# TensorE order within a slot: the output product between gate and value, and unit outputs behind the multiplication

## Chip, cores and metric

The kernel runs on one core of a Trainium2 chip. The metric is the time of one execution on the device in microseconds (us). Where two kernels are compared, the ratio is the mean time of one kernel's fast runs over that of the other's of the same rounds, so it is not quite the ratio of the medians quoted beside it.

## The reference

An attention block with 32 learned queries is followed by a gated feed-forward block; the second one takes nearly all of the time.

```python
h = mab(I, x)                    # 32 inducing rows attend to 12416 rows, 4 batches
x = mab(x, h)                    # every row attends to the 32 rows of h
rms = sqrt(mean(x * x, -1) + 1e-6); xn = x / rms * rms_g
g = xn @ w_gate                  # 128 -> 1536
silu = g / (1 + exp(-g))
val = xn @ w_val                 # 128 -> 1536
out = (silu * val) @ w_out       # 1536 -> 128, 49664 rows
```

## The kernel before

The rows are cut into 100 units of at most 512 columns, and each unit into 12 slots (`j`), one for each 128 of the 1536 channels. A slot makes a gate and a value product on TensorE (single-pass `float32r`), a silu on ScalarE, a multiplication `u` on VectorE, and one output product of some earlier slot. An output product is either plain (`float32`, which TensorE runs as two passes: 1598 matmul records for 799 products) or split into three single passes, for which ScalarE and GpSimd make `hi`, `lo` and `d`. Attention work of the next batch is spread over the slots as planned steps.

```python
ps_gv = pool("ps_gv", 4, space=PSUM)      # gate and value products share four banks
...
def project(lhsT, rhs):
    nc.tensor.matmul(acc[:, 0:T], lhsT, rhs, start=..., stop=...)
    st["left"] -= 1
    if not st["left"]:                     # last output product of the unit
        o = ...
        nc.vector.tensor_tensor(out=o, in0=acc, in1=o, op=ALU.add)      # shortened
        nc.vector.transpose(out=o[:, 0:T], in_=...)
        soon(2, lambda: store(o))
...
for j in range(NJ):
    g = ps_gv.tile(...); nc.tensor.matmul(g, sg[:, ts(j, P)], a)        # L597
    v = ps_gv.tile(...); nc.tensor.matmul(v, sv[:, ts(j, P)], a)        # L599
    sl = silp.tile(...); nc.scalar.activation(sl, g, AF.Silu)           # L601
    t = up.tile(...);    nc.vector.tensor_tensor(out=t, in0=sl, in1=v)  # L603
    slot(j)            # steps that are due, planned steps, then one or two output products
```

A planned step splits the rows of a stack into two halves, all on VectorE:

```python
nc.vector.transpose(out=aT[rows, 0:w], in_=sc[b][rows, cols2[s]])       # L500
nc.vector.tensor_copy(out=hi[rows, 0:w], in_=aT[rows, 0:w])             # L502
nc.vector.tensor_tensor(out=lo, in0=aT, in1=hi, op=ALU.subtract)        # L503
```

## Time and profile before

| | before |
|---|---|
| time, median of 3 runs | 1718.8 us (1718.05 to 1718.83) |
| TensorE busy | 1680.2 us, 98% of the span |
| VectorE, ScalarE, GpSimd busy | 70%, 70%, 69% |
| quiet slot with a plain output product | 1.327 us |
| quiet slot with a split output product | 1.16 us |

The first row is what is measured without a profile; the rest is from one profiled execution. TensorE's busy share alone does not prove that it is the bound, since a busy matmul row can hold queueing.

### The profile page before, as it was taken

Reading aid. Unit: us, or ns where it says so; the run is one execution under the profiler, and the core shown is the slowest. Engines: PE = TensorE matmul, PEld = TensorE weight load, DVE = VectorE, ACT = ScalarE, POOL = GpSimd, SP = SyncE. Lnnn points to the kernel's source line nnn. Section 1 sums busy time; section 2 is a strip of 40 time slices with the busy share of each in tenths; the row PEclk is TensorE's granted clock in tenths of the full one; section 3 lists DMA queues with packets and bytes.
Section 4 is the critical chain, followed back from the end, with each engine's and each line's share of the span. In section 5 each row is a group of like instructions: output and inputs, shape, how many; then the busy total and the mean of one; then the engine's idle time right before and its main releaser. Section 6 shows DMA issues by size and latency. Waiting matters only on the chain.

```text
span 1716.6 us, 23555 instructions
## 1 busy us (share of the span) xinstructions
PE 1680.2 (98%) x6855; PEld 1045.7 (61%) x6855; DVE 1201.7 (70%) x1982; ACT 1207.7 (70%) x2180; POOL 1179.0 (69%) x936
## 2 busy tenths in 40 slices
PE   9899999999999999999999999999999999999998
PEld 7545565655566656665656656565556666666666
DVE  4867876777578776667667877667757666766665
ACT  4347777676677777766777777767677777787776
POOL 0317775777487776676657877577647888888875
PEclk9999999999999999999999999999999999999999
DMA  6344433434343232434434324153211121121121
GB/s 248 86 68 74 72 78 71 110 77 70 55 80 62 50 67 47 105 76 90 68 58 83 55 37 84 41 121 79 51 30 34 33 37 31 33 36 36 32 36 24
DMA packets 389360, 112.66 MB, mean 66 GB/s; under 512 B 365136, under 2 KB 369776, under 8 KB 386672
## 3 DMA queue, kind: packets, MB, share of 16 engines
q1 hardware_dynamic: 388944, 111.02, 32.3%
q8 instruction: 54, 0.88, 0.2%
q14 instruction: 74, 0.61, 0.1%
q10 hardware_dynamic: 288, 0.15, 0.0%
HBM read 53.95 MB, written 27.00 MB: 47 GB/s over the span
## 4 chain that ended last, share of the span: by engine, by line
PE 91%; ACT 3%; DVE 2%; issue 2%; DMA 1%; POOL 1%; ACTq 0%; DVEq 0%; POOLq 0%
PE acc L550 42%; PE gv L599 16%; PE gv L597 16%; PE u L563 5%; PE u L565 5%; PE mm L301 3%; ACT silu L601 1%; PE mm L478 1%; DVE u L603 1%; PE mm L358 1%; DMA xn<-in_x_dram 1%; PE acc L178 1%; ACT L601 1%; PE gv L358 0%; PE mm L430 0%
## 5 line engine op out<-in xcount | busy, mean ns | idle before, releaser
L603 DVE TENSOR_TENSOR u<-silu,gv 128x512 f32<-128x512 f32 (+2 forms) x1200 | 785.7, 665 | 444.6 <-ACT silu L601 378.3
L601 ACT ACTIVATE silu<-gv 128x512 f32<-128x512 f32 (+2 forms) x1200 | 699.5, 585 | 414.7 <-PE gv L597 357.9
L550 PE MATMUL acc<-u,wo 128*128 128x512 f32 (+2 forms) x1598 | 797.3, 583 | 0.1
L597 PE MATMUL gv<-a,sg 128*128 128x512 f32 (+2 forms) x1200 | 768.3, 640 | 14.6 <-ACT silu L601 6.6
L585 POOL TENSOR_TENSOR xn<-u,xn 128x512 fp32r<-128x512 f32 (+2 forms) x401 | 505.9, 1262 | 309.7 <-ACT xn L584 250.0
L590 POOL TENSOR_TENSOR xn<-hs,xn 128x512 fp32r<-128x512 f32 (+2 forms) x401 | 507.8, 1266 | 74.0 <-POOL xn L585 25.6
L599 PE MATMUL gv<-a,sv 128*128 128x512 f32 (+2 forms) x1200 | 475.7, 396 | 5.2 <-DVE u L603 3.3
L597 PEld LDWEIGHTS gv<-a,sg 128*128 128x128 f32 x1200 | 227.6, 190 | 223.4 <-issue 140.5
L599 PEld LDWEIGHTS gv<-a,sv 128*128 128x128 f32 x1200 | 228.1, 190 | 214.5 <-issue 125.7
L550 PEld LDWEIGHTS acc<-u,wo 128*128 128x128 f32 x1598 | 295.4, 189 | 93.5 <-issue 33.8
L584 ACT ACTIVATE xn<-u 128x512 fp32r<-128x512 f32 (+2 forms) x401 | 245.7, 613 | 17.6 <-DVE u L603 16.0
L589 ACT ACTIVATE hs<-xn 128x512 f32<-128x512 f32 (+2 forms) x401 | 246.3, 614 | 7.1 <-POOL xn L590 6.9
L563 PE MATMUL u<-xn,xn 128*128 128x512 f32 (+2 forms) x401 | 167.9, 419 | 0.0
L550 PE MATMUL acc<-xn,xn 128*128 128x512 f32 (+2 forms) x401 | 156.1, 389 | 2.4 <-POOL xn L590 2.4
L565 PE MATMUL u<-xn,xn 128*128 128x512 f32 (+2 forms) x401 | 155.4, 387 | 0.0
L563 PEld LDWEIGHTS u<-xn,xn 128*128 128x128 f32 x401 | 75.2, 188 | 43.2 <-issue 26.3
L492 POOL TENSOR_TENSOR rs<-ms,mhalf 128x16 f32<-128x16 f32 (+2 forms) x28 | 75.5, 2698 | 36.2 <-DVE ms L490 35.7
L565 PEld LDWEIGHTS u<-xn,xn 128*128 128x128 f32 x401 | 75.4, 188 | 19.1 <-issue 5.2
L550 PEld LDWEIGHTS acc<-xn,xn 128*128 128x128 f32 x401 | 75.3, 188 | 18.8 <-POOL xn L590 2.9
L555 DVE TENSOR_TENSOR o<-acc,o 128x512 f32<-128x512 f32 (+2 forms) x97 | 65.1, 671 | 21.7 <-ACT o L568 18.9
L556 DVE STREAM_TRANSPOSE o<-o 128x512 f32<-128x512 f32 (+2 forms) x97 | 67.7, 698 | 3.3
L568 ACT ACTIVATE o<-u 128x512 f32<-128x512 f32 (+2 forms) x97 | 56.4, 582 | 19.0 <-PE u L565 16.7
(155 smaller groups left out, 758.0 us busy)
## 6 DMA issues: line engine op xcount, KB each, us to landing
out_dram<-o SPq DMA_DIRECT2D x320, 64.0 KB, 2.0
xT<-in_x_dram SPq DMA_DIRECT2D x60, 256.0 KB, 4.5
xn<-in_x_dram SPq DMA_DIRECT2D x60, 256.0 KB, 4.7
a<-hi SPq DMA_DIRECT2D x160, 64.0 KB, 2.0
a<-lo SPq DMA_DIRECT2D x158, 64.0 KB, 2.0
w<-w SPq DMA_DIRECT2D x22, 256.0 KB, 3.3
xn<-in_x_dram SPq DMA_DIRECT2D x5, 1024.0 KB, 11.2
out_dram<-o SPq DMA_DIRECT2D x64, 60.0 KB, 2.0
```

Of the source, the lines that this page charges most:

```text
L492: nc.gpsimd.tensor_tensor(out=rs, in0=ms, in1=mhalf[rows, 0:n], op=ALU.pow)
L550: nc.tensor.matmul(acc[:, 0:T], lhsT, rhs, start=st["left"] == NJ, stop=st["left"] == 1)
L563: nc.tensor.matmul(ups[:, 0:T], w[:, i, :], hi, start=st["k"] == nk, stop=False)
L565: nc.tensor.matmul(ups[:, 0:T], w[:, NK + i, :], lo, start=False, stop=not st["k"])
L584: nc.scalar.activation(hi, v, AF.Copy, scale=1.0 - 2.0 ** -13)
L585: nc.gpsimd.tensor_tensor(out=lo, in0=v, in1=hi.bitcast(F32), op=ALU.subtract)
L589: nc.scalar.activation(hs[:, 0:T], hi.bitcast(F32), AF.Copy, scale=2.0 ** -12)
L590: nc.gpsimd.tensor_tensor(out=d, in0=hs[:, 0:T], in1=lo.bitcast(F32), op=ALU.subtract)
L597: nc.tensor.matmul(g[:, 0:T], sg[:, ts(j, P)], a[:, 0:T], start=True, stop=True)
L599: nc.tensor.matmul(v[:, 0:T], sv[:, ts(j, P)], a[:, 0:T], start=True, stop=True)
L601: nc.scalar.activation(sl[:, 0:T], g[:, 0:T], AF.Silu)
L603: nc.vector.tensor_tensor(out=t[:, 0:T], in0=sl[:, 0:T], in1=v[:, 0:T], op=ALU.mult)
```

## The change

The intent is to start the value product as late as its multiplication can use it: the silu takes about 0.6 us, and meanwhile the output product runs, so the value product sits in its PSUM bank for a shorter time. For this `slot` is parted in two: `products` (the output products) comes between gate and value, `steps` (all else) after the multiplication. The addition and transpose that end a unit would then stand on VectorE ahead of the slot's own multiplication, so they are put off to the `steps` that follow.

```diff
-                o = st["o"] if nk else outp.tile([P, 512], F32, name="o")
-                if nk:
-                    nc.vector.tensor_tensor(...)
-                nc.vector.transpose(...)
-                soon(2, lambda: store(o))
+                soon(1, finish)
+
+        def finish():
+            ... # the same lines
@@
             nc.tensor.matmul(g[:, 0:T], sg[:, ts(j, P)], a[:, 0:T], start=True, stop=True)
+            sl = silp.tile([P, 512], F32, name="silu")
+            nc.scalar.activation(sl[:, 0:T], g[:, 0:T], AF.Silu)
+            products(j)
             v = ps_gv.tile([P, 512], F32, name="gv", tag="gv")
             nc.tensor.matmul(v[:, 0:T], sv[:, ts(j, P)], a[:, 0:T], start=True, stop=True)
-            sl = silp.tile([P, 512], F32, name="silu")
-            nc.scalar.activation(sl[:, 0:T], g[:, 0:T], AF.Silu)
             t = up.tile([P, 512], F32, name="u")
             nc.vector.tensor_tensor(out=t[:, 0:T], in0=sl[:, 0:T], in1=v[:, 0:T], op=ALU.mult)
-            slot(j)
+            steps(j)
```

(`slot` becomes `steps`, which runs what is due and what is planned, and `products`, whose counting is unchanged.) `soon(1, ...)` reads as "a slot later", which is misleading here: `finish` is registered by `products(j)` and runs in `steps(j)` of the same slot, with the steps that are due and so ahead of those that are planned.

More of the change, by code (lines that the diff above doesn't have):

```diff
@@ L535, in split_wo, with ffn @@
             kws[name] = xnp.tile([P, 4, 512], F32R, name=f"xn{full - 4 + k}")
-    def ffn(b, u, slot):
+    def ffn(b, u, products, steps):
         s, q = units[u]
@@ L552, in project @@
             if not st["left"]:
-                o = st["o"] if nk else outp.tile([P, 512], F32, name="o")
-                if nk:
-                    nc.vector.tensor_tensor(out=o[:, 0:T], in0=acc[:, 0:T], in1=o[:, 0:T], op=ALU.add)
-                nc.vector.transpose(out=o[:, 0:T], in_=(o if nk else acc)[:, 0:T])
-                soon(2, lambda: store(o))
+                soon(1, finish)
+        def finish():
+            o = st["o"] if nk else outp.tile([P, 512], F32, name="o")
+            if nk:
+                nc.vector.tensor_tensor(out=o[:, 0:T], in0=acc[:, 0:T], in1=o[:, 0:T], op=ALU.add)
+            nc.vector.transpose(out=o[:, 0:T], in_=(o if nk else acc)[:, 0:T])
+            soon(2, lambda: store(o))
         def project3(j, hi, lo, d):
@@ L795, with steps @@
         for u in range(NU):
-            def slot(j):
+            def steps(j):
                 k = u * NJ + j
-                now = b * NU * NJ + k
                 for one in waiting:
                     one[0] -= 1
-                for one in [one for one in waiting if not one[0]]:
+                while any(not one[0] for one in waiting):
+                    one = next(one for one in waiting if not one[0])
                     waiting.remove(one)
@@ L812, in slot, with products @@
                     gather(*after[b, u])
+            def products(j):
+                k = u * NJ + j
+                now = b * NU * NJ + k
                 count = max(len(plain) - 1, 0) + sum(at <= now for at, _ in kara)
@@ L823, in slot @@
                         plain.pop(0)()
-            ffn(b, u, slot)
+            ffn(b, u, products, steps)
     while kara or plain:
         (plain.pop(0) if plain else kara.pop(0)[1])()
-    for _, step in waiting:
-        step()
+    while waiting:
+        waiting.pop(0)[1]()
 _INS = ['x', 'inducing', 'moe_w_gate', 'moe_w_val', 'moe_w_out', 'moe_rms_g']
```

## The prediction

> **What bounds the kernel now.** I read the page first: busy shares, then the chain that ended last, then the costliest groups.
>
> ```profile
> PE 1680.2 (98%) x6855; PEld 1045.7 (61%) x6855; DVE 1201.7 (70%) x1982; ACT 1207.7 (70%) x2180; POOL 1179.0 (69%) x936
> ...
> PE 91%; ACT 3%; DVE 2%; issue 2%; DMA 1%; POOL 1%; ACTq 0%; DVEq 0%; POOLq 0%
> ...
> L603 DVE TENSOR_TENSOR u<-silu,gv 128x512 f32<-128x512 f32 (+2 forms) x1200 | 785.7, 665 | 444.6 <-ACT silu L601 378.3
> ...
> L597 PE MATMUL gv<-a,sg 128*128 128x512 f32 (+2 forms) x1200 | 768.3, 640 | 14.6 <-ACT silu L601 6.6
> ...
> L599 PE MATMUL gv<-a,sv 128*128 128x512 f32 (+2 forms) x1200 | 475.7, 396 | 5.2 <-DVE u L603 3.3
> ```
>
> TensorE is busy for 98% of the span and carries 91% of the last chain; no other engine is over 70%. VectorE's 378.3 us of waiting for the silu lies on an engine that is not the bound. A busy matmul row can still hide waits, so I looked at a quiet stretch of the timeline.
>
> ```profile
> 805.36 1.02 PE L550 MATMUL acc<-u,wo 128*128 128x512 f32 x2
> ...
> 805.82 0.80 PE L597 MATMUL gv<-a,sg 128*128 128x512 f32 x1
> ...
> 806.46 0.40 PE L599 MATMUL gv<-a,sv 128*128 128x512 f32 x1
> ...
> 806.69 1.02 PE L550 MATMUL acc<-u,wo 128*128 128x512 f32 x2
> ...
> 807.15 0.80 PE L597 MATMUL gv<-a,sg 128*128 128x512 f32 x1
> ```
>
> From gate to gate a slot takes 807.15 - 805.82 = 1.33 us. The value product starts 0.23 us before the output product, which has two passes. By unrounded starts each pass lasts 0.429 and gate and value 0.235 each: 2 x 0.429 + 2 x 0.235 = 1.328. The sum fills the slot, so TensorE streams without a hole. (The gate's row starts early and reads 0.80 because it is queued behind the second output pass.) With a split output product (L563, L565, L550, three single passes) five single passes take 1.16 us.
>
> How much of the run is not like this? I took all value-product starts from the trace and grouped the slots by what TensorE runs in them. The 530 plain slots of width 512 last 707.7 us in all and are together 4.9 us longer than if each had the group's 10th percentile; the 264 split ones last 318.5 us, excess 12.3. Over all slots, real waiting comes to about 57 us: 18 before 142 us (the weights are being prepared), about 21 around the two long exponentials of each of three batches, 6 in the four narrow units (256 columns), 8.5 in ten stalls of 0.6 to 0.9 us, and the rest in slots without an output product. Of the ten stalls this is one:
>
> ```profile
> 1374.21 1.66 DVE L503 TENSOR_TENSOR lo<-aT,hi 128x512 fp32r<-128x512 f32 x1
> ...
> 1375.79 2.58 DVE L603 TENSOR_TENSOR u<-silu,gv 128x512 f32<-128x512 f32 x4
> ...
> 1376.52 0.50 PE L597 MATMUL gv<-a,sg 128*128 128x512 f32 x1 [0.65 <-DVE u L603]
> ```
>
> VectorE was held by a slow split (1.66 us), the multiplications queued behind it, and TensorE found no free bank. Such stalls are what the change can shorten.
>
> **What the Trainium skill says.** "TensorE: Matmul & The Clock Gate", section Step-by-step, says that matmuls stay in program order while weight loads are pulled ahead of running matmuls. The trace agrees: weight loads of 0.19 us lie beside the stream (PEld 61% busy). So an order of products costs nothing by itself if the same kinds of pass follow one another. Its section Back-to-back issue gap gives about 216 ns for 512 columns; this trace has 235 for a single pass and 429 for each fp32 pass, and I use these. "PSUM — Partial Sum Buffer", Specifications, has 8 banks per partition; the kernel takes all (4 gate and value, 2 accumulators, 1 + 1), so the change has only the order in which to relieve a bank. "GPSIMD Engine Reference", Specifications, says that its SBUF interfaces are shared with VectorE when VectorE has two SBUF inputs; the 1.66 us split, which takes 0.69 elsewhere in this trace (at 265.41), fits.
>
> **The change part by part.** It adds and removes no arithmetic instruction.
>
> 1. *TensorE order.* Before: gate, value, two output passes. After: gate, two output passes, value. In steady state both are the same cycle: two single passes, then two fp32 passes; only the names of the single ones change places. I expect 1.33 and 1.16 us a slot again. Change: 0.
>
> 2. *The value bank is held shorter.* In the trace the silu starts 0.43 us after its gate, where the gate was not queued, and takes 0.60: it ends 1.03 us after the gate starts. The multiplication starts 0.83 us (median) after the value product does (0.43 would do if the silu were there). Before: value at 0.235, multiplication 1.07 to 1.75, so the bank is held 1.5 us. After: value at 0.235 + 0.86 = 1.09, multiplication 1.52 to 2.2, bank held 1.1 us. The next use of a bank, two slots on, is at 2 x 1.33 + 0.235 = 2.9 before and 3.75 after: slack goes from 1.1 to 1.5 us. Of ten stalls totalling 8.5 us I take off about 0.4 us each, with some gone: about -5 us. After an exponential the first value product no longer stands behind the multiplication (about 0.25 us, six times): -1 us.
>
> 3. *Less slack from a multiplication to its output product.* The product is issued 0.235 us earlier relative to its gate and the multiplication ends 0.4 to 0.45 us later: 0.65 us less, and up to 1.2 us less where attention products are in the slot, as those now come after the output product. I followed the kernel's own queue: plain products run 2 slots behind 41 times, 3 slots 485 times, 4 or more 271 times; split ones 5 or 6 behind. In the trace the slack from multiplication to product has a median of 2.8 us, 5th percentile 0.94, 1st 0.39. Shifting each by these amounts makes 26 plain products late by 7 us together; most follow an exponential, when the queue is drained. The split products' GpSimd result has slack 0.67 at the 5th percentile; shifting makes three newly late by 0.5 us each. Around 130 to 137 us TensorE already waits for GpSimd, and the value product now stands behind that wait: +0.5. Together about +6 us, of which a part replaces a wait that is there anyway: +4.
>
> 4. *Unit outputs.* 97 units have an addition (671 ns) and a transpose (698 ns). They go ahead of the planned steps rather than after them, and behind the last value product's multiplication. The 1.4 us on VectorE stay; they delay the next multiplication by about 0.7 us instead of 0.55, within the new slack. Change: 0.
>
> Sum: 0 - 6 + 4 + 0 = -2 us; from 1718.8 that is about 1717.
>
> **The rivals.**
>
> *A real gain.* If the shorter hold also dissolved the stalls of the exponentials and the narrow units, 8.5 + 6 + half of 21 could go: 25 us, 1694 us (1.5%). For it: many weight loads wait for silu or multiplication. Against it: most of these waits are 0.24 us long, under a running fp32 pass, and behind an exponential TensorE waits for ScalarE, which stays blocked as long, with the same number of banks ahead of it. Over 2% is 34 us; that needs more waits than I can find.
>
> *A new wait.* Gate and value banks come from one pool of four, and 201 of the 1200 gate weight loads wait for VectorE (value banks), not for ScalarE. For these the multiplication now ends at 2.2 us and the gate is due at 2.65, in split slots at 2.32; the load must be clear 0.2 us before. If more gates drew such banks, each could lose 0.1 to 0.2 us: 200 of them 20 to 40 us, 1740 to 1755 us. Against it: banks are handed out as they come free, and the silu's comes first.
>
> *VectorE becomes the bound.* It has 70% now and gets no new work, but the multiplication is no longer ready until the slot's end. If transposes wait behind it, attention steps slip. With 30% idle and planned steps several slots apart I give it 5 us at most.
>
> **Range and chances.** The terms are -6 and +4, each uncertain by about its own size, and the engines' contention shifts by a few us whenever order changes. Repeated times lie within 0.8 us, so noise adds nothing. I take 1716, slightly under the start, and 1704 to 1729 for 8 in 10. Outside the 2% band: 0.04 faster, 0.03 slower.
>
> **What would show it.** In quiet stretches the slot should stay at 1.33 and 1.16 us; another figure makes step 1 wrong. The value row should read about 0.80 us in the mean rather than 0.40, and the gate row 0.40: queueing only. VectorE's wait before the multiplication should be laid to the value product (PE) instead of the silu. Ten stalls near 199, 614, 1027 and 1375 to 1685 us should shrink to 0.5 or vanish (step 2). Output products should show short waits for VectorE after the exponentials near 277, 452, 691 and 866 us (step 3). The prediction fails if the quiet slot changes, or if gate weight loads wait for VectorE's multiplication far more than the 22.3 us that the view of waits has now.

## The result, and the profile after

The changed kernel takes 1717.7 us (median of 4 runs, 1717.4 to 1718.2), the kernel before 1718.4 in its runs up to then (4, 1715.7 to 1718.8). The ratio is 1.000 with a 95% interval of 0.998 to 1.002: the same time.

Two rows of the page before are needed for comparison, those of the output products (plain, then the last product of a split one):

```profile
L550 PE MATMUL acc<-u,wo 128*128 128x512 f32 (+2 forms) x1598 | 797.3, 583 | 0.1
...
L550 PE MATMUL acc<-xn,xn 128*128 128x512 f32 (+2 forms) x401 | 156.1, 389 | 2.4 <-POOL xn L590 2.4
```

The page of the changed kernel, busy shares and costliest groups (the columns are busy us and mean ns, then the idle time of the engine before them and what ended most of it):

```profile
PE 1675.3 (98%) x6855; PEld 1046.2 (61%) x6855; DVE 1189.4 (69%) x1982; ACT 1222.4 (71%) x2180; POOL 1181.4 (69%) x936
...
L607 DVE TENSOR_TENSOR u<-silu,gv 128x512 f32<-128x512 f32 (+2 forms) x1200 | 788.2, 665 | 471.9 <-PE gv L605 276.6
...
L550 PE MATMUL acc<-u,wo 128*128 128x512 f32 (+2 forms) x1598 | 793.9, 581 | 7.0 <-DVE u L607 5.8
L605 PE MATMUL gv<-a,sv 128*128 128x512 f32 (+2 forms) x1200 | 768.1, 640 | 1.3 <-ACT silu L602 0.7
...
L600 PE MATMUL gv<-a,sg 128*128 128x512 f32 (+2 forms) x1200 | 492.5, 410 | 14.3 <-ACT silu L602 6.5
...
L550 PE MATMUL acc<-xn,xn 128*128 128x512 f32 (+2 forms) x401 | 159.0, 396 | 6.2 <-POOL xn L593 5.9
```

Gate and value have changed rows: the value's row now reads 640 ns, the gate's 410. That is queueing behind the second output pass, not work. VectorE's longest wait is laid to the value product instead of the silu. TensorE's idle time before gate and value is 15.6 us (19.8 before), but output products, which hardly waited before (0.1 and 2.4 us), now wait 7.0 and 6.2 us. By these rows idle time rose from 22.3 to 28.8 us, while TensorE's busy time fell by 4.9 us; as busy rows hold queueing, the page alone doesn't say what was won or lost.

A quiet stretch of the changed kernel's timeline (start and duration in us, then engine and line):

```profile
804.84 0.40 PE L600 MATMUL gv<-a,sg 128*128 128x512 f32 x1
...
805.07 1.02 PE L550 MATMUL acc<-u,wo 128*128 128x512 f32 x2
...
805.11 0.69 DVE L607 TENSOR_TENSOR u<-silu,gv 128x512 f32<-128x512 f32 x1 [0.84 <-PE gv L605]
...
805.53 0.80 PE L605 MATMUL gv<-a,sv 128*128 128x512 f32 x1
...
806.17 0.40 PE L600 MATMUL gv<-a,sg 128*128 128x512 f32 x1
```

From gate to gate it is 806.17 - 804.84 = 1.33 us, as before. The order is another, the stream is as full.

To see where the few us went I took the end of every slot's gate product in both traces and watched the difference (changed less before) grow along the slots. The numbers are in us; a minus is a gain.

| slots of a batch | where | batches 0, 1, 2 |
|---|---|---|
| 0 to 48 of the first batch | weights are being prepared | -0.86 |
| 132 to 144 | first long exponential | -0.25, -0.26, -0.23 |
| 192 to 204 | planned products | -0.45, -0.46, -0.46 |
| 204 to 216 | a split product waits for GpSimd | +0.74, +0.74, +0.74 |
| 228 to 240 | a split product waits for GpSimd | +0.90, +0.89, +0.90 |
| 252 to 264 | second long exponential | -1.80, -0.55, -1.59 |
| 0 to 12 of the next batch | | -0.35, -0.39, -0.31 |

These sum to -3.1 us, losses of 4.9 included. The other stretches add 1.2 up to slot 1188, in steps of under 0.3, and the end of the program 0.9. The spans differ by 1.0 (1716.65 and 1715.69).

### The profile page after: what moved, and what is told of

Same layout as the page of the kernel before. It is cut to its first block, busy times and chain, and to the rows that moved or that the text cites. A ratio compares the mean times of both kernels' runs of the same rounds, so it can differ in the third digit from the quotient of the medians.

```text
span 1715.7 us, 23430 instructions
## 1 busy us (share of the span) xinstructions
PE 1675.3 (98%) x6855; PEld 1046.2 (61%) x6855; DVE 1189.4 (69%) x1982; ACT 1222.4 (71%) x2180; POOL 1181.4 (69%) x936
## 5 line engine op out<-in xcount | busy, mean ns | idle before, releaser
L605 PE MATMUL gv<-a,sv 128*128 128x512 f32 (+2 forms) x1200 | 768.1, 640 | 1.3 <-ACT silu L602 0.7
L593 POOL TENSOR_TENSOR xn<-hs,xn 128x512 fp32r<-128x512 f32 (+2 forms) x401 | 507.0, 1264 | 53.4 <-POOL xn L588 16.7
L600 PE MATMUL gv<-a,sg 128*128 128x512 f32 (+2 forms) x1200 | 492.5, 410 | 14.3 <-ACT silu L602 6.5
L550 PEld LDWEIGHTS acc<-u,wo 128*128 128x128 f32 x1598 | 299.1, 189 | 87.5 <-issue 17.9
L568 PE MATMUL u<-xn,xn 128*128 128x512 f32 (+2 forms) x401 | 155.8, 388 | 0.0
L566 PE MATMUL u<-xn,xn 128*128 128x512 f32 (+2 forms) x401 | 155.4, 388 | 0.0
L566 PEld LDWEIGHTS u<-xn,xn 128*128 128x128 f32 x401 | 75.3, 188 | 15.6
```

The source lines that it names most:

```text
L550: nc.tensor.matmul(acc[:, 0:T], lhsT, rhs, start=st["left"] == NJ, stop=st["left"] == 1)
L566: nc.tensor.matmul(ups[:, 0:T], w[:, i, :], hi, start=st["k"] == nk, stop=False)
L568: nc.tensor.matmul(ups[:, 0:T], w[:, NK + i, :], lo, start=False, stop=not st["k"])
L593: nc.gpsimd.tensor_tensor(out=d, in0=hs[:, 0:T], in1=lo.bitcast(F32), op=ALU.subtract)
L600: nc.tensor.matmul(g[:, 0:T], sg[:, ts(j, P)], a[:, 0:T], start=True, stop=True)
L605: nc.tensor.matmul(v[:, 0:T], sv[:, ts(j, P)], a[:, 0:T], start=True, stop=True)
```

## The experiments

Each kernel ran five rounds (the two with three banks ran three) beside the kernel before, which had a median of 1718.07, 1717.91 and 1717.96 us in the three calls. By the verdicts' mark of 2% every run with four banks is "the same" as the kernel before; the smaller differences below rest on the intervals in brackets. A comparison with the changed kernel itself (1717.7) is one across calls.

### The order alone

```diff
-                soon(1, finish)
+                finish()
```
(in the changed kernel)

> The new TensorE order alone; the unit's addition and transpose stay right behind the last output product, so on VectorE they now come before that slot's multiplication. Theory (TensorE is a full stream, the order is worth nothing, and a multiplication has slack): 97 multiplications end about 0.5 us later than in the changed kernel, 2.7 + 0.7 = 3.4 us after their gate against a bank need at 3.75 (3.2 in split slots), so 0 to 10 us longer than the changed kernel, 1717 to 1728. Rival (moving the unit outputs gave back what the order cost, so the order alone is clearly slower): over 1735.

It took 1722.6 us (1721.7 to 1722.8), ratio to the kernel before 1.0025 (1.0012 to 1.0037). The estimate holds: 4.9 us over the changed kernel. By the difference of gate ends to the changed kernel the losses come late in each of three batches: 1.06 us in slots 236 to 248, 0.4 around and behind the second exponential (up to slot 272), 0.7 in the last units (up to 296). Earlier in each batch some is won back (0.5 at slots 132 to 144, 0.3 at 228 to 240). In the page output products wait for the multiplication 8.9 us instead of 5.8. So the putting-off of unit outputs is a necessary part of the change.

### The unit outputs alone

```diff
-                o = ...   # addition, transpose and store of the unit, at once
+                soon(1, finish)
```
(in the kernel before; there it does mean a slot later)

> The old TensorE order with the unit outputs one slot later on VectorE. Theory: 1716 to 1720, since VectorE has 30% idle and the 1.4 us per unit only change places. Rival (unit outputs block multiplications in the kernel before, and this part carries a gain that the order takes back): 1700 to 1710.

It took 1721.7 us (1721.2 to 1723.6), ratio 1.0024 (1.0011 to 1.0036). That is 1.7 us over what I expected at the most, and the rival is refuted: this part carries no gain. In the old order it costs, for instance because the stalls of 0.90 us in the last batch become 1.15 us each. So both parts cost about 4 us alone and nothing together. Why these stalls grow, the traces show. In the kernel before:

```profile
1372.60 1.30 POOL L590 TENSOR_TENSOR xn<-hs,xn 128x512 fp32r<-128x512 f32 x1
...
1373.19 0.98 DVE L502 CAST hi<-aT 128x512 fp32r<-128x512 f32 x1
```

and with the unit outputs a slot later:

```profile
1374.18 1.29 POOL L593 TENSOR_TENSOR xn<-hs,xn 128x512 fp32r<-128x512 f32 x1
...
1374.54 1.21 DVE L502 CAST hi<-aT 128x512 fp32r<-128x512 f32 x1
```

In both, VectorE's cast ends about 0.28 us after the GpSimd subtraction beside it (1373.90 and 1374.17; 1375.47 and 1375.75); a cast with no GpSimd operation beside it takes 0.43 us. Counted from the gate product that starts just before this row of steps (1371.66 and 1373.00), the cast starts equally late in both kernels (1.53 and 1.54 us), but the subtraction starts at 1.18 us instead of 0.94, and all that follows on VectorE is 0.24 us later. Why GpSimd is later is not shown.

### Three banks instead of four

```diff
-    ps_gv = pool("ps_gv", 4, space=PSUM)
+    ps_gv = pool("ps_gv", 3, space=PSUM)
```
(in the kernel before, and in the changed one)

> The kernel before with 3 instead of 4 banks for gate and value products. By due times: the gate two slots on draws a value bank, multiplication ends at 1.75 us and the gate is due at 2.65 (2.32 in split slots), the value at 2.9 needs the silu that ends at 2.4. No wait in quiet stretches, more where VectorE or ScalarE is late: 10 to 30 us over the kernel before, 1728 to 1750.

> The changed kernel with 3 banks. If holding the value bank 0.4 us shorter is what counts when banks are scarce (the change's intent), it loses less than the kernel before with 3 banks: below it by 5 us or more. If the later end of the multiplication counts (2.2 us against a gate due at 2.65, 2.32 in split slots, weight load 0.2 us earlier), it loses more: split slots wait about 0.1 us each, and every late VectorE step shows, so 10 to 40 us over the other 3-bank kernel.

The kernel before took 1782.0 us with three banks (ratio 1.0375, 1.0360 to 1.0391), the changed one 1750.5 (1.0189, 1.0175 to 1.0203; at the 2% mark slower for the first, unclear for the second). The loss is 64 us in one and 33 us in the other. Groups of the kernel before with three banks (idle time of TensorE at the end of the line):

```profile
L599 PE MATMUL gv<-a,sv 128*128 128x512 f32 (+2 forms) x1200 | 481.8, 402 | 57.1 <-ACT silu L601 32.7 <-DVE u L603 20.6 <-DVE eT L472 2.1
```

and of the changed kernel with three banks:

```profile
L605 PE MATMUL gv<-a,sv 128*128 128x512 f32 (+2 forms) x1200 | 762.6, 636 | 23.0 <-ACT silu L602 12.4 <-DVE u L607 10.4
L600 PE MATMUL gv<-a,sg 128*128 128x512 f32 (+2 forms) x1200 | 497.7, 415 | 14.8 <-DVE u L607 8.8 <-ACT silu L602 4.1 <-DMA a<-lo 1.5
```

The value product's waits for a bank fall from 57.1 to 23.0 us. This is the most telling pair: the intent of the change is sound and is worth about 31 us where banks are scarce. (Some 4 us of it may be clock: after 145 us the trace of the first has four windows of 3.41 us at half clock, that of the second none; a window is estimated at 1.1 us under "Luck" below.) My due-time argument, by which the changed kernel should have lost more, is refuted, and the size of the first loss was underestimated twofold. With four banks the waits that the shorter hold could remove are hardly there.

### All split products due a slot later

```diff
-            ready[b, u, j] = int((free + 0.3) / SLOT) + 1
+            ready[b, u, j] = int((free + 0.3) / SLOT) + 2
```
(in the changed kernel, and in the kernel before)

> The changed kernel, split output products due one slot later. Theory: the waits of TensorE for GpSimd's last difference that are new after the change (in slots 205 to 228 and 229 to 240 of each of three batches, 0.74 and 0.90 us, 4.9 us in all) vanish, as a slot is 1.2 us and the lateness about 1 us; the output products' waits for GpSimd in the page fall from 5.9 to below 3 us (the one of 2.9 us near 132 us shrinks too). Time 3 to 7 us below the changed kernel: 1711 to 1715. Rival (those waits only move the place where TensorE catches up): same time within 1 us.

> The control: the kernel before, split output products due one slot later. It has only the wait of 2.45 us near 133 us for GpSimd, so theory says 0 to 3 us below the kernel before (1715 to 1718) and less gain than with the changed kernel. If it gains as much as the changed kernel does (5 us), the later due date helps by something else than the new waits.

The changed kernel took 1723.4 us (ratio 1.0039, 1.0026 to 1.0053), the kernel before 1729.0 (1.0062, 1.0049 to 1.0076): both slower, which neither theory said. The waits for GpSimd did go: the split products' idle time fell from 5.9 to 1.4 us. But the edit does a second thing. Following the queue's rules I find 60 slots without an output product instead of 36, and 58 with two instead of 34; in the empty ones TensorE outruns ScalarE and VectorE and waits for banks (in the changed kernel the idle time before gate and value rises from 15.6 to 22.6 us). The experiment was too blunt. One thing can be read from the pair: the changed kernel loses 5.4 us less than the kernel before ((1729.0 - 1717.9) - (1723.4 - 1717.7) = 5.4), close to the 4.9 us of new waits that only the changed kernel had to lose.

### Two split products per batch due a slot later

```diff
-            ready[b, u, j] = int((free + 0.3) / SLOT) + 1
+            ready[b, u, j] = int((free + 0.3) / SLOT) + 1 + (b < B - 1 and k in (209, 230))
```
(in the changed kernel; these two are the ones that TensorE waits for)

> The changed kernel with only the two split products per batch that TensorE waits for (made in slots 209 and 230 of three batches) due one slot later. By the queue's own rules the number of slots without (36) and with two output products (34) stays, unlike in the run where all were due later (60 and 58). Theory: six waits, 3 x (0.74 + 0.90) = 4.9 us, go: 3 to 5 us below the changed kernel, 1712.5 to 1715. Rival (the wait returns in the next slot): within 1 us of the changed kernel.

It took 1713.1 us (1712.5 to 1713.6), ratio 0.9971 (0.9959 to 0.9984), 4.6 us below the changed kernel. The difference of gate ends to the changed kernel falls by 0.72, 0.71 and 0.71 us at slots 204 to 216 and by 0.90, 0.89 and 0.90 us at 228 to 240 of the three batches, and nowhere near as much elsewhere after the first 50 slots. The new waits for GpSimd are real, cost what they seemed to cost, and don't come back later.

### Unit outputs behind the planned steps

```diff
-                soon(1, finish)
+                late.append(finish)
@@ end of steps(j)
+                while late:
+                    late.pop(0)()
```
(in the changed kernel)

> The changed kernel, but the unit's addition and transpose come behind the slot's planned steps instead of ahead of them (same slot). Theory: in the changed kernel they push a planned reduction on VectorE back by 1.4 us (near 416 us and at the same place in the next two batches), GpSimd's subtraction waits for it, the split product's last difference comes late and TensorE waits 0.90 us. With the order turned round these three waits vanish: 2 to 4 us below the changed kernel, 1713.5 to 1716, with the waits of 0.74 us (slots 205 to 216) unchanged. Rival (GpSimd's lateness there comes from the new TensorE order alone): the waits of 0.90 stay, and the time is the changed kernel's within 1 us.

It took 1715.0 us (1714.0 to 1715.4), ratio 0.9982 (0.9969 to 0.9994), 2.7 us below the changed kernel; the waits of the second place go (slots 228 to 240: 0.88, 0.87 and 0.88 us), those of the first stay. The timelines show the chain. In the changed kernel:

```profile
415.51 0.68 DVE L558 TENSOR_TENSOR o<-acc,o 128x512 f32<-128x512 f32 x1
416.23 0.71 DVE L559 STREAM_TRANSPOSE o<-o 128x512 f32<-128x512 f32 x1
...
416.86 0.64 DVE L409 TENSOR_REDUCE mx<-sc 128x16 f32<-128x512 f32 x1
...
417.59 1.05 POOL L410 TENSOR_TENSOR sc<-sc,mx 128x512 f32<-128x512 f32 x1 [1.26 <-PE gv L600]
418.59 1.28 POOL L593 TENSOR_TENSOR xn<-hs,xn 128x512 fp32r<-128x512 f32 x1
...
419.93 0.50 PE L550 MATMUL acc<-xn,xn 128*128 128x512 f32 x1 [0.60 <-POOL xn L593]
```

The unit's addition and transpose stand ahead of the planned maximum (L409); GpSimd, which subtracts it, sits idle for 1.26 us (the view blames a gate product, but what it lacked was the maximum, as the other order shows), then makes the last difference of the split product (L593) too late for TensorE. In the other order:

```profile
416.32 0.68 DVE L409 TENSOR_REDUCE mx<-sc 128x16 f32<-128x512 f32 x1
416.92 0.68 DVE L558 TENSOR_TENSOR o<-acc,o 128x512 f32<-128x512 f32 x1
417.10 1.04 POOL L410 TENSOR_TENSOR sc<-sc,mx 128x512 f32<-128x512 f32 x1
```

GpSimd follows on at once, with no idle time noted.

### The cast of the stack's split on ScalarE

```diff
-            nc.vector.tensor_copy(out=hi[rows, 0:w], in_=aT[rows, 0:w])
+            nc.scalar.copy(out=hi[rows, 0:w], in_=aT[rows, 0:w])
```
(in the changed kernel, and in the kernel before)

> The changed kernel with the first half of the stacked split (the cast) on ScalarE. The ten stalls of 0.5 to 0.9 us that the change left as they were come, by my reading, from three VectorE steps in a row (transpose, cast, difference; 0.7 + 0.5 + 1.7 us) in front of a multiplication. Taking the cast out lets the multiplications start about 0.5 us earlier: stalls near 198, 612, 1026, 1373, 1435, 1498, 1560 and 1623 us fall from 0.85 to 0.3 or so, together 4 to 6 us, 1712 to 1714. Rival (ScalarE, at 71%, delays the silu by as much and the difference waits for ScalarE anyway): no gain, 1717 to 1722.

> Control for the cast on ScalarE, in the kernel before. If the ten stalls come from VectorE's three steps in a row whatever the order of TensorE, the gain is the same 5 us as with the changed kernel: 1711.5 to 1714.5. If the changed order was needed for it, less than 2 us: 1716 to 1718.

The changed kernel took 1712.6 us (1712.3 to 1714.3), ratio 0.9971 (0.9959 to 0.9984): 5.1 below itself. The kernel before took 1714.3 (1713.8 to 1714.6), ratio 0.9978 (0.9966 to 0.9991): 3.6 below itself. The stalls lose about 0.5 us each in the first case and 0.4 in the second, so VectorE's row of steps takes part in them in either order. The changed kernel's stall, which was to shrink by the change and didn't:

```profile
1371.20 0.70 DVE L500 STREAM_TRANSPOSE aT<-sc 128x512 f32<-128x512 f32 x1
...
1371.94 0.50 DVE L502 CAST hi<-aT 128x512 fp32r<-128x512 f32 x1
...
1372.48 1.66 DVE L503 TENSOR_TENSOR lo<-aT,hi 128x512 fp32r<-128x512 f32 x1
...
1374.06 1.27 DVE L607 TENSOR_TENSOR u<-silu,gv 128x512 f32<-128x512 f32 x2
...
1374.79 0.51 PE L600 MATMUL gv<-a,sg 128*128 128x512 f32 x1 [0.68 <-DVE u L607]
```

and the same place with the cast on ScalarE:

```profile
1371.50 0.70 DVE L500 STREAM_TRANSPOSE aT<-sc 128x512 f32<-128x512 f32 x1
...
1372.24 0.62 ACT L502 CAST hi<-aT 128x512 fp32r<-128x512 f32 x1 [1.42 <-DVE aT L500]
...
1372.89 0.69 DVE L503 TENSOR_TENSOR lo<-aT,hi 128x512 fp32r<-128x512 f32 x1 [0.68 <-ACT hi L502]
...
1373.41 0.51 PE L600 MATMUL gv<-a,sg 128*128 128x512 f32 x1 [0.16 <-ACT silu L602]
```

The size was right and the reason only half of it. The difference (L503) starts no earlier after its transpose (1.39 us against 1.28), but takes 0.69 us instead of 1.66, because no GpSimd subtraction runs beside it now.

### All three together

The changed kernel with the cast on ScalarE, the unit outputs behind the planned steps, and the two split products due later.

> The changed kernel with the cast on ScalarE, the unit outputs behind the planned steps and the two split products due later. If the gains are of different waits: 5 for the cast, 4.9 for the six waits (the unit outputs' order then adds nothing more to these): 1706 to 1710, below both kernels by about half a per cent. If they overlap: 1711 to 1713.

It took 1708.2 us (1707.6 to 1708.6), ratio 0.9943 (0.9930 to 0.9957): 0.57% below the kernel before. The gains of the cast (5.1) and of the late waits (4.6) add up: 9.6 us below the changed kernel. Against the kernel before with the cast alone it is 6.2 us faster (1714.3 - 1708.2). It is the fastest version that I have, and it beats both kernels.

## Why the prediction was right, point by point

**The time** came out as said: 1717.7 against 1716, inside the range, the same within 2%. Step 1, the 0 on which all else rests, held. That the small terms met their sum was partly luck: in the two traces the gains of the table come to 8.0 us (about 2.3 of them the half clock below) against the -6 of step 2, but hardly in the places that it names, and the losses come to 4.9 us, of which 2.2 belong to step 3 (+4) and 2.7 to step 4 (0).

**Step 1 (order, 0 us)** held. Over all slots of width 512 the median is 1.327 us for plain ones in both traces (530 and 534 slots), and 1.160 before and 1.165 after for split ones (264 each).

**Step 2 (bank held shorter, -6 us)** was right in mechanism and wrong in its main place. The hold did fall, from about 1.5 to 1.2 us (the value product recorded at 804.20 us starts 0.41 us later, when the output pass ahead of it is through, and its multiplication ends at 805.11 + 0.69 = 805.80), and with three banks that is worth 31 us. But the claim "Of ten stalls totalling 8.5 us I take off about 0.4 us each" failed. Measured as the length of the slot over the usual one, the three of 0.85 to 0.88 us near 200, 614 and 1027 us changed by 0.02 at most, and those after 1370 us shrank by 0.04 to 0.07 (first four) and by about 0.3 (those near 1625 and 1685): about 0.8 us in all, not 5. In the stall shown above it is a gate, not a value product, that waits for the multiplication, because the four banks are one pool and the value product had taken a bank that a silu had freed. Both kernels get to the end of the same slot before they stop, so a value bank filled later helps nothing. What came instead, about 0.25 us at each first exponential and 0.55 at a second one at full clock, fits the small second term of that step (-1 us) in place and comes to about 2.4 us for six, over twice as much; no experiment took it apart. The 0.45 us at slots 192 to 204 of three batches is in no step.

**Step 3 (less slack to the output product, +4 us)** held in mechanism. Output products wait 5.8 us for the multiplication where none was noted before: six waits of 0.20 to 0.23 us behind the exponentials, as forecast, and three of about 0.97 us, near 492, 905 and 1319 us, where it was a value or gate product that waited 0.81 to 0.92 us before, so that these replace a wait; the rest lies at the two ends of the program. And the three splits "newly late by 0.5 us each" are the ones at slot 214, late by 0.74 us each, because the output product now comes before the attention products of its slot. The later due date for two splits a batch took these away.

**Step 4 (unit outputs, 0 us)** was wrong at one place. "They go ahead of the planned steps rather than after them" was seen and taken to cost nothing; it delays one planned maximum by 1.4 us, GpSimd behind it, and TensorE by 0.90 us in each of three batches: 2.7 us, which the reversed order gave back. VectorE's share of busy time (70%) could not show this: the cost lay in what was queued behind the unit's output and in who waited for it.

**The rivals.** A real gain did not come. The new wait through banks came only in the weight loads: of the 1200 gate weight loads 270 are set to wait for VectorE now, 201 before. The view of waits has, before (us in total, times, longest):

```profile
PEld gv L597 <- DVE u L603: 22.3, 53, 1.3
...
PE gv L597 <- DVE u L603: 6.4, 11, 0.9
```

and after:

```profile
PEld gv L600 <- DVE u L607: 46.9, 125, 1.1
...
PE gv L600 <- DVE u L607: 6.2, 10, 0.7
```

So the sign that the prediction named for its own failure, weight loads that wait far more than 22.3 us, did come (46.9), and the prediction did not fail: the loads run beside other matmuls, and the gate matmuls idle no longer than before (6.2 and 6.4 us). It was a badly chosen sign. (The rival's sum was a little off too: 20 to 40 us on 1718.8 make 1739 to 1759.) VectorE did not become the bound (69% busy).

**A reading of the skill.** The 216 ns that the prediction quotes from "Back-to-back issue gap" is there the gap of an isolated matmul; for a stream of loads and matmuls the same section has about 131 ns. The trace's 235 ns for a single pass is above both. Nothing rests on it, as the prediction worked with 235 and 429.

**Luck.** Part of the gain around the second exponential comes with a lower clock in the trace before: the kernel before ran at half clock for 3.41 us there in two batches of three, and lost an estimated 1.1 us each time (1.80 and 1.59 against 0.55). These are the windows of four us in the kernel before around it, in its first and third batch:

```profile
core 0: us, PE busy (x) PEld busy (x) DVE busy (x) ACT busy (x) POOL busy (x), PEclk, DMA share, GB/s
452.00:456.00 4.00, 4.00 (x10) 2.14 (x11) 3.27 (x7) 1.99 (x5) 0.30 (x1) 0.70 0.21 31
...
1279.00:1283.00 4.00, 4.00 (x9) 2.00 (x10) 2.70 (x6) 1.41 (x4) 0.12 (x1) 0.58 0.42 61
```

The seventh figure after the window is the granted clock, 0.70 and 0.58; in the changed kernel it is 1.00 in the same stretches (452 to 458 and 1279 to 1285 us). Two us is the size of all that the change moved, so a single pair of profiles can't tell such a difference. Of the 27 runs of the kernel before beside the experiments, the eleven with the mean clock of the four changed ones (0.996) have a mean of 1717.8 us, and so have the four. Whether the order takes part in the clock stays open: after 145 us and before the end, three of the five traces with the old order have such a fall of the clock, and none of the eight with the new order (three banks included). The prediction's 0.8 us for the spread of repeated times was small: four runs of the kernel before lie 3.1 us apart.

## What to carry to other kernels

When an engine already streams without holes, a change of order is worth only the waits that it takes away, and these are counted slot by slot, not from busy shares or from the idle time of other engines. A buffer held for a shorter time pays where buffers are scarce (31 us with three banks) and nothing measurable where they are not (four banks). Work that is put ahead of planned steps on a half-idle engine can still cost, if another engine waits for one of those steps: look at who is behind it in the queue.

## What the Trainium skill lacked or had wrong

- "TensorE: Matmul & The Clock Gate", LDWEIGHTS, gives the number of columns divided by 1.2 in ns, 107 ns for 128 columns; the weight loads here take 190 ns in the mean (1200 gate loads, f32 words).
- The same page, What's actually happening, lets the clock fall to half after an idle window of about 3.4 us. Here it fell for 3.41 us about 2 us after a stall in which TensorE's matmuls were idle for 0.97 us and its weight loads for 1.75, in two batches of three; in the third the same stall of 0.97 us left it at full clock. Its section on a second failure mode says that short idle gaps can make the clock fall too; how much idle time is enough it doesn't say.
- "GPSIMD Engine Reference", Specifications, names the contention with VectorE instructions that have two SBUF inputs; its row has no size (other pages of the skill say more of it). The same 128x512 difference took 1.66 us beside a GpSimd subtraction (which took 1.47 instead of about 1.28) and 0.69 us beside none. The cast in front of it took 0.43 us beside none and 0.5 to 1.3 us where a subtraction had over 0.15 us left to run, and then ended 0.26 to 0.29 us after the subtraction's end, in all four traces looked at (both kernels, the order alone, the outputs alone).
- No page says that the gate product of one slot can be held by the value bank of another where both come from one pool: here 201 (before) and 270 (after) of 1200 gate loads are set to wait for VectorE.
